# Attention steps of batches 2 to 7 in another order, and k's maxima spread by DMA instead of by TensorE

## The chip, the cores and the metric

One core of one Trainium2 chip runs the whole program. The metric is the device time of one execution in microseconds (us). The kernel before takes 855.56 us, the median of three runs (854.65 to 856.44).

Five engines work side by side, each through its own list of instructions in a fixed order: TensorE (PE in the profile; PEld are its weight loads), VectorE (DVE), ScalarE (ACT), GpSimd (POOL) and SyncE (SP), which here only issues DMAs. An instruction that waits holds up all that stands behind it on its engine.

## The reference

```
q_s = exp(q - max over d);  q_s = q_s / (sum over d + 1e-9)
k_s = exp(k - max over s);  k_s = k_s / (sum over s + 1e-9)
kv  = einsum('bhsd,bhse->bhde', k_s, v)
x   = einsum('bhsd,bhde->bhse', q_s, kv)        # 8 batches, 8 heads, 576 rows, 64 columns
x   = x, heads side by side: 4608 x 512
h   = x @ w_in                                  # 512 -> 2048
out = (h * erf(softplus(h))) @ w_out            # 2048 -> 512
```

Note that k's maximum is taken over the 576 rows, which lie on partitions: it has to be brought to every partition before it can be subtracted.

## The kernel before

**The network (MoE) part** is the bulk of the work. The 4608 tokens are cut into 12 blocks of 384, three for each pair of batches, and the 2048 hidden columns into four groups. One item `n` is one block with one group; there are 48 of them. For an item, `mm1(n, k)` with k = 0 to 3 (L975, matmuls at L999) makes `H_n` in PSUM tiles `pY`, `pX`, `pZ`, each product being 12 matmuls of 128x192; each of the three tiles has one buffer, so a product waits until the one before it in that tile has been read. DVE reads some of them (L1011, L1013, L1021, L1024), ACT the others (L1016, L1018, L1026). Then `softplus` and `erf` run on ACT (L344, each with a table load), `gmul`, `ghi` and `glo` on DVE (L1079, L1093, L1097), and two items later `mm2(n, tt)` with tt = 0 to 2 (L1125, 12 matmuls of 128x512 each) adds into `o`. Operands are split into two fp16 halves, so that three fp16 products stand for one of fp32. The first items (0 to 5) use fp32 for `mm2` (L1116), and while items 4 to 8 run, the weights are still being split (L297, L298) and combined (L322).

**The attention part** makes the tokens `x`, one batch after another. Batches 0 and 1 are written in fp32 and aren't touched by the change. Batches 2 to 7 go through the generator `attention16(b)` (L649), whose steps are:

- `k_max` (L492): DVE takes maxima over each partition's own rows into `kmax`; `k_max_T` (L504): TensorE transposes `kmax` into bank `kT` (L508) and DVE reduces it to `km`, 4 numbers on each of 128 partitions (L512); `k_max_rows` (L517): TensorE transposes `km`, broadcast, into bank `kB` (L521), so that each partition has all 512 maxima in PSUM.
- `q_sub` (L451): row maxima of q and their subtraction (L454, L455); then k minus `kB` (L662, L667), and the exponentials on ACT (L344).
- `kv_mm` and `kv_norm` (L528, L554): k'v of four heads each (`kv_b_0`, `kv_b_1`; L542), its normalization into `kvf` (L565).
- `q_norm` and `q_halves` (L459, L636): q divided by its sums, split into fp16 halves (ACT L640, DVE L641, placed over the k half that k'v has used up), and transposed by a DMA.
- `kv_max` (L576) and `kv_split` (L584): the largest entry of `kvf` (`mx`, L578) is spread over the partitions by a transpose on TensorE into `x_bk` (L125), reduced by DVE (L127), made into a scale, and with it `kvf` is split into `kvbd` (L595, L596), the operand of the next step.
- `x_mm` (L632): for odd batches first the rest of both batches' rows (`xt`), then four products `x_b_0` to `x_b_3`; ACT moves them into the blocks `x` (L443). After `x_b_1` and `x_b_3` the loads of the next batch's q halves are issued, after k'v those of its k and v.

**What sets the order.** After each step the generator yields a share; `pace` (L1207), called after every `mm2`, takes further steps until the sum of shares has reached a goal that rises evenly with `n`. The shares are the table `SHARES16` (L49). The code order this gives is then put through a list scheduler, which fixes each engine's list of instructions by its own estimate of when each is ready. All loads, stores and DMA transposes are issued from SP's one list. The attention banks (`kT`, `kB`, `kv`, `x_bk`, `xt`, `x`) share two PSUM buffers.

The main loop, for items 4 and up:

```
for i in range(4):
    if m0: tok(f"m{n}.{i}")                       # mm1, quarter i of item n
    if 4 < n <= N and i < 2 and n - 1 not in OUT32: tok(f"{'IO'[i]}{n - 1}")
    if m2 and i < 3:
        tok(f"M{n - 2}.{i}")                      # mm2 of item n - 2
        pace(n + (i + 1) / NTT)                   # attention steps
```

Of the kernel before, what the change touches and what calls it, by code (L numbers as in the profile page):

```python
# [45 lines left out]
OUTS = [2, 3, 0, 1]  # L46

SHARES = [2.51, 0, 0.16, 0.09, 1.58, 2.43, 1.12, 0.26, 0.29, 0.04, 0.78, 1.12, 0.16]
SHARES16 = [2.51, 0, 0.16, 0.09, 1.58, 2.43, 1.3, 2.43, 1.3, 0.26, 0.3, 0.78, 0.3]  # L49
LEAD = 2.0  # L50

EXPMASK = 0x7F800000
# [5 lines left out]
def attn_moe_kernel(  # L58
# [18 lines left out]
    NC4 = DM // P  # L77
# [261 lines left out]
    def act(out_, in_, func, chain=True, **kw):  # L339

        with ExitStack() as es:
            if chain and last[0] is not None:
                es.enter_context(tc.issue_after(last[0]))
            i = nc.scalar.activation(out_, in_, func, **kw)  # L344
# [100 lines left out]
    def hd(t):  # L445
        return t.rearrange("p h d -> p (h d)")

    def rows(t):
        return t.rearrange("p t h d -> p (t h) d")

    def q_sub(t, g, name):  # L451

        m = at.tile([P, g], F32, tag=f"qm{g}", bufs=1, name=f"{name}_m")
        nc.vector.tensor_reduce(m, t, axis=AX.X, op=ALU.max)  # L454
        nc.vector.tensor_tensor(  # L455
            t, t, m[:, :, None].to_broadcast([P, g, D]), op=ALU.subtract
        )
# [58 lines left out]

    def k_max_rows(b, km):  # L517

        bk = bank(f"kB_{b}")
        for c in range(NC4):  # L520
            nc.tensor.transpose(  # L521
                bk[:, c * P:(c + 1) * P], km[:, c:c + 1].to_broadcast([P, P]), ident
            )
# [30 lines left out]
    def kv_norm(b, hf, bk):  # L554
        if b >= E32:
            if hf == 0:
                bat[b]["kvf"] = at.tile([P, NC4, D], F32, tag="qT", name=f"kvf_{b}")
            kvf = bat[b]["kvf"]
        bkv = bk[:, :2 * W].rearrange("p (c w) -> p c w", c=2)
        rd = at.tile([P, 2, 1], F32, tag="rd", bufs=1, name=f"rd_{b}_{hf}")  # L560
        nc.vector.tensor_scalar_add(rd, bkv[:, :, D:], 1e-9)
        nc.vector.reciprocal(rd, rd)
        cs = slice(2 * hf, 2 * hf + 2)
        if b >= E32:
            nc.vector.tensor_tensor(  # L565
                kvf[:, cs, :], bkv[:, :, :D], rd.to_broadcast([P, 2, D]), op=ALU.mult
            )
            return
        for a in range(2):
            ps = slice(a * D, (a + 1) * D)  # L570
            nc.vector.tensor_tensor(
                kv32[b][ps, cs, ps], bkv[ps, :, :D], rd[ps].to_broadcast([D, 2, D]),
                op=ALU.mult,
            )

    def kv_max(b):  # L576
        mx = at.tile([P, 1], F32, tag="mx", bufs=1, name=f"mx_{b}")
        nc.vector.tensor_reduce(  # L578
            mx, (kv32[b] if b < E32 else bat[b]["kvf"]).rearrange("p c e -> p (c e)"), axis=AX.X,
            op=ALU.max, apply_absolute_value=True,  # L580
        )
        return mx
# [50 lines left out]
                out_, kvbd[b % 2][:, wl, c, :], qT[:, ql], start=(i == 0), stop=(i == 2)  # L633
            )

    def q_halves(src, place, name):  # L636

        n = src.shape[1]
        st_ = place.bitcast(F16).rearrange("p (i n) -> p i n", i=2)
        nc.scalar.copy(st_[:, 0], src)  # L640
        nc.vector.tensor_tensor(st_[:, 1], src, st_[:, 0], op=ALU.subtract)  # L641
        qT = src.bitcast(F16).rearrange("p (a s) -> p a s", s=P)
        nc.sync.dma_start_transpose(qT, place.bitcast(F16))
        return qT.rearrange("p (i a) s -> p i a s", i=2)

    def flat3(t):
        return t.rearrange("p a b c -> p (a b c)")

    def attention16(b):  # L649
        d, j, p = bat[b], b % 2, b // 2  # L650
        even = bat[b - j]
        tl = slice(j * TAIL, (j + 1) * TAIL)
        ks, qs, kt = d["k"], d["q"], even["kt"][tl]
        sh = iter(SHARES16)
        kmax = k_max(b, ks, (kt, tl))
        yield next(sh)
        km = k_max_T(b, kmax)
        q_sub(rows(qs[0]), 16, f"q_{b}_0")
        yield next(sh)
        kb = k_max_rows(b, km)  # L660
        for hf in range(2):
            nc.vector.tensor_tensor(  # L662
                ks[hf], ks[hf],
                kb[:, None, hf * 4:hf * 4 + 4, :].to_broadcast([P, TM, 4, D]),
                op=ALU.subtract,
            )
        nc.vector.tensor_tensor(kt, kt, kb[tl], op=ALU.subtract)  # L667
        yield next(sh)
        q_sub(rows(qs[1]), 16, f"q_{b}_1")
        if j == 1:  # L670
            q_sub(even["qt"], H, f"qt_{p}")
        yield next(sh)
        for t in (*ks, kt, qs[0], qs[1], *([even["qt"]] if j == 1 else [])):
            act(t, t, AF.Exp, chain=b > 1)
        yield next(sh)
        qT = {}
        for hf in range(2):
            kv_norm(b, hf, kv_mm(b, hf))
            if hf == 0:
                d["v"].append(load_half(v, "v", b, 1))  # L680
            q_norm(rows(qs[hf]), 16, f"q_{b}_{hf}", b)
            yield next(sh)
            qT[hf] = q_halves(flat3(qs[hf]), flat3(ks[hf]), f"{b}_{hf}")
            yield next(sh)
        if j == 1:
            q_norm(even["qt"], H, f"qt_{p}", b)
            qT[2] = q_halves(hd(even["qt"]), hd(even["kt"]), f"{p}_t")
        if b + 1 < B:
            load_kv(b + 1)
        mx = kv_max(b)  # L690
        yield next(sh)
        kv_split(b, mx)
        yield next(sh)
        for i in ((3 * p + 1, 3 * p + 2) if j else (3 * p, 3 * p + 1)):
            while not x_free(i):
                yield 0
        w = next(sh)
        if j == 1:
            bk = bank(f"xt_{p}")
            x = xblock(p * NBK + 1)  # L700
            bk3 = bk.rearrange("p (c s) -> p c s", c=NC4)
            for a in range(2):
                for c in range(NC4):
                    cs = slice(a * TAIL, (a + 1) * TAIL)
# [571 lines left out]
```

## Time and profile before

| | |
|---|---|
| three runs | 854.65, 855.56, 856.44 us |
| the profiled execution | 855.05 us, of which the profile's span is 852.9 us |
| TensorE (PE) | busy 813.8 us, 95% of the span |
| VectorE (DVE) | busy 633.3 us, 74% |
| ScalarE (ACT) | busy 503.5 us, 59% |
| DMA | 62.59 MB, 73 GB/s on average |
| granted TensorE clock | 0.992 |

The span is what the profile can see; 2.1 us of the execution lie around it. An engine's busy share is an average over stages. Items 0 to 3 and batches 0 and 1 fill about the first 130 us, items 4 to 8 with the weights' splitting go to about 205 us, and from there on an item follows an item with batches 2 to 7 woven in, until about 700 us, where the attention has ended and only the network part goes on. Rows of the timeline have the start in us from the span's start, the duration, engine, line, operation, what is written and what is read, and the count of like instructions merged; in square brackets stands how long the engine was idle before it and which instruction released it.

### The profile page before, as it was taken

The page shows a single profiled execution, that of the slowest core. Times are in us where ns is not written, and L with a number is a line of the kernel's source. Part 1 is how long each engine was busy: PE and PEld are TensorE (multiplying, and loading weights), DVE is VectorE, ACT ScalarE, POOL GpSimd, SP SyncE. Part 2 cuts the span into 40 slices and gives each one's busy share as a digit, 9 for nine tenths or more (in the row PEclk, how much of TensorE's full clock was granted, in tenths as well). Part 3 has the DMA queues.
Part 4 walks back from the last instruction along what each step waited for, and adds up shares of the span by engine and source line. Part 5 has one row for each costly group of instructions (what it writes and reads, how often), then busy time and mean ns, then how long its engine had stood idle before and what let it go on. Part 6 is the DMA issues. An engine that isn't in the chain of part 4 may idle for free.

```text
span 852.9 us, 15321 instructions
## 1 busy us (share of the span) xinstructions
PE 813.8 (95%) x6424; PEld 554.2 (65%) x6424; DVE 633.3 (74%) x909; ACT 503.5 (59%) x633; POOL 17.6 (2%) x37
## 2 busy tenths in 40 slices
PE   2999997999999999999999999999999999999997
PEld 1655546666667667766777676766776676777673
DVE  5899979999995879758865779758866656553543
ACT  2598486876674656645663566555664465553532
POOL 2010000000000000000000000000000000000000
PEclk8899999999999999999999999999999999999999
DMA  9996420043326303412134302412131000000100
GB/s 250 409 251 194 123 63 25 7 85 66 87 51 130 98 3 64 99 31 50 49 85 86 91 10 51 97 46 51 33 55 38 31 9 1 38 2 1 38 2 37
DMA packets 145508, 62.59 MB, mean 73 GB/s; under 512 B 134688, under 2 KB 136736, under 8 KB 145440
## 3 DMA queue, kind: packets, MB, share of 16 engines
q1 hardware_dynamic: 143264, 53.23, 25.1%
q0 software_dynamic: 2176, 8.39, 2.7%
q8 instruction: 50, 0.82, 0.4%
q14 instruction: 18, 0.15, 0.1%
HBM read 45.09 MB, written 9.44 MB: 64 GB/s over the span
## 4 chain that ended last, share of the span: by engine, by line
PE 52%; DVE 25%; ACT 14%; issue 4%; SPq 2%; DMA 2%; ACTq 0%; POOL 0%; DVEq 0%
PE o L1125 25%; PE pX L999 13%; PE pZ L999 6%; ACT G L344 6%; ACT L344 5%; DVE G L1079 3%; PE pY L999 3%; DVE H L1097 2%; SPq L409 2%; DVE H L1093 2%; PE kv L542 2%; DVE x L298 1%; PE x L632 1%; DVE x L388 1%; PE o L1116 1%
## 5 line engine op out<-in xcount | busy, mean ns | idle before, releaser
L1125 PE MATMUL o<-wo,H 128*128 128x512 f16 x1512 | 348.0, 379 | 1.7 <-DVE H L1093 1.3
L999 PEld LDWEIGHTS <-wi 128*128 128x128 f16 x3696 | 309.1, 98 | 46.3 <-issue 18.5
L1125 PEld LDWEIGHTS <-H 128*128 128x128 f16 x1512 | 145.7, 98 | 150.0 <-DVE H L1093 1.8
L999 PE MATMUL pX<-x,wi 128*128 128x192 f16 x2112 | 204.8, 247 | 7.7 <-ACT H L1018 4.1
L344 ACT ACT_TABLE_LOAD x104 | 133.4, 1283 | 4.7 <-DVE H L1024 2.8
L1079 DVE SCALAR_TENSOR_TENSOR G<-G,small,H 128x1536 f32<-128x1536 f32 x44 | 80.0, 1817 | 60.9 <-ACT G L344 60.6
L1026 ACT COPY H<-pX 128x384 f32<-128x384 f32 x44 | 20.9, 474 | 163.4 <-PE pX L999 163.4
L999 PE MATMUL pZ<-x,wi 128*128 128x192 f16 x1056 | 103.8, 246 | 1.4 <-DVE H L1024 1.0
L344 ACT ACTIVATE G<-H,U 128x768 f32<-128x768 f32 (+1 forms) x60 | 72.7, 1231 | 22.1 <-DVE H L1024 21.5
L1097 DVE TENSOR_TENSOR H<-G,H 128x1536 f16<-128x1536 f32 x42 | 73.8, 1756 | 1.0
L344 ACT ACTIVATE G<-G 128x1536 f32<-128x1536 f32 x48 | 71.2, 1484 | 0.5
L1116 PE MATMUL o<-wo,G 128*128 128x512 f32 x144 | 66.6, 602 | 0.0
L999 PE MATMUL pY<-x,wi 128*128 128x192 f16 x528 | 51.2, 246 | 1.6 <-DVE H L1011 1.6
L1024 DVE TENSOR_TENSOR H<-pZ,H 128x384 f32<-128x384 f32 x44 | 24.4, 554 | 32.1 <-PE pZ L999 32.1
L1011 DVE COPY H<-pY 128x384 f32<-128x384 f32 x44 | 24.4, 555 | 30.7 <-PE pY L999 30.7
L1116 PEld LDWEIGHTS o<-wo,G 128*128 128x128 f32 x144 | 26.1, 192 | 25.8 <-issue 25.1
L297 ACT ACTIVATE x<-x 128x768 f16<-128x768 f32 (+1 forms) x44 | 32.7, 761 | 14.3 <-DVE x L388 14.2
L1093 DVE CAST H<-G 128x1536 f16<-128x1536 f32 x42 | 40.2, 957 | 0.8
L1141 DVE TENSOR_SCALAR ob<-o,V 128x512 f32<-128x512 f32 x29 | 21.7, 748 | 25.6 <-PE o L1125 25.6
L298 DVE SCALAR_TENSOR_TENSOR x<-x,x 128x768 f16<-128x768 f32 (+1 forms) x44 | 37.1, 852 | 3.4 <-ACT x L297 3.4
L443 ACT ACTIVATE x<-x 128x384 f32<-128x384 f32 (+1 forms) x52 | 17.6, 391 | 32.0 <-PE x L632 29.5
L1013 DVE TENSOR_TENSOR H<-pX,H 128x384 f32<-128x384 f32 x44 | 24.5, 556 | 14.6 <-PE pX L999 14.3
(184 smaller groups left out, 769.0 us busy)
## 6 DMA issues: line engine op xcount, KB each, us to landing
out_dram<-ob SPq DMA_DIRECT2D x32, 256.0 KB, 2.4
vbuf<-in_v_dram SPq DMA_DIRECT2D x60, 128.0 KB, 3.1
q<-in_q_dram SPq DMA_DIRECT2D x56, 128.0 KB, 3.2
k<-in_k_dram SPq DMA_DIRECT2D x56, 128.0 KB, 3.2
wo<-in_moe_w_in_dram SPq DMA_DIRECT2D x4, 1024.0 KB, 17.0
wi<-in_moe_w_out_dram POOLq DMA_DIRECT2D x2, 1024.0 KB, 8.0
wi<-in_moe_w_in_dram SPq DMA_DIRECT2D x2, 1024.0 KB, 8.8
raw<-in_moe_w_out_dram POOLq DMA_DIRECT2D x2, 1024.0 KB, 7.9
```

The costliest lines, as they stand in the source:

```text
L297: nc.scalar.activation(hi, src, AF.Copy, scale=s)
L298: nc.vector.scalar_tensor_tensor(lo, src, s, hi, op0=ALU.mult, op1=ALU.subtract)
L344: i = nc.scalar.activation(out_, in_, func, **kw)
L999: nc.tensor.matmul(o, w[wl][:, c, a * P:(a + 1) * P], x[:, xl, xi, c, :], start=(new and a == 0 and c == 0 and i == 0), stop=(c == 1 and i ...
L1011: nc.vector.tensor_copy(C[0, 0], bank2("Y"))
L1013: add(C[0, 0], bank2("X"), C[0, 0], op=ALU.add)
L1024: add(C[0, 1], bank2("Z"), C[0, 1], op=ALU.add)
L1079: nc.vector.scalar_tensor_tensor(flat(s["G"]), flat(s["G"]), (GB if n in OUT32 else GA)[:, g:g + 1], flat(s["H"]), op0=ALU.mult, op1=ALU.mult,
L1093: nc.vector.tensor_copy(flat(s["gh"]), flat(s["G"]))
L1097: nc.vector.tensor_tensor(flat(s["gl"]), flat(s["G"]), flat(s["gh"]), op=ALU.subtract)
L1116: nc.tensor.matmul(o, s["G"][:, a, ts_], w[:, a, :], start=(first_ and a == 0), stop=(last_ and a == FG - 1),)
L1125: nc.tensor.matmul(o, s[gt][:, a, ts_], w[wl][:, a, :], start=(first_ and a == 0 and i == 0), stop=(last_ and a == FG - 1 and i == 2),)
```

## The change

Three things are changed for batches 2 to 7.

1. `k_max_rows` is replaced by `k_max_spread`: `km` is written by a DMA to a row of 512 numbers in DRAM (4 bytes to a packet), and a second DMA reads that row back, repeated for each of the 128 partitions, into an SBUF tile `kB`. Both are issued from SP, and the second waits for the first. Four transposes on TensorE for each batch go, and the subtraction (now L672, L677) reads SBUF where it read PSUM.
2. The steps stand in another order: maxima, their transposing and the two DMAs are one step; then `q_sub` of both halves, and k's subtraction after them; the first q half stands behind `kv_b_0`, and the second one behind `kv_b_1`, `kv_max` and `kv_split`, which stood behind both q halves.
3. The shares are new numbers, written at each step, and `SHARE16` is their sum.

```
+    def k_max_spread(b, km):
+        row = dr.tile([1, DM], F32, tag="km", name=f"kmd_{b}")
+        nc.sync.dma_start(row.rearrange("o (c p) -> (o p) c", c=NC4), km)
+        kb = at.tile([P, DM], F32, tag="qT", name=f"kB_{b}")
+        nc.sync.dma_start(kb, row.to_broadcast([P, DM]))
+        return kb.rearrange("p (h d) -> p h d", h=H)
...
-        kmax = k_max(b, ks, (kt, tl))
-        yield next(sh)
-        km = k_max_T(b, kmax)
+        kb = k_max_spread(b, k_max_T(b, k_max(b, ks, (kt, tl))))
+        yield 1.8
         q_sub(rows(qs[0]), 16, f"q_{b}_0")
-        yield next(sh)
-        kb = k_max_rows(b, km)
+        yield 0.9
+        q_sub(rows(qs[1]), 16, f"q_{b}_1")
+        if j == 1:
+            q_sub(even["qt"], H, f"qt_{p}")
+        yield 0.9
         for hf in range(2):
             nc.vector.tensor_tensor(
...
+        def q_half(hf):
             q_norm(rows(qs[hf]), 16, f"q_{b}_{hf}", b)
-            yield next(sh)
-            qT[hf] = q_halves(flat3(qs[hf]), flat3(ks[hf]), f"{b}_{hf}")
-            yield next(sh)
+            yield 0.75
+            qT[hf] = q_halves(flat3(qs[hf]), flat3(ks[hf]))
+            yield 0.75
+
+        kv_norm(b, 0, kv_mm(b, 0))
+        d["v"].append(load_half(v, "v", b, 1))
+        yield 0.4
+        yield from q_half(0)
+        kv_norm(b, 1, kv_mm(b, 1))
+        mx = kv_max(b)
+        yield 0.6
+        kv_split(b, mx)
+        yield 0.4
+        yield from q_half(1)
...
-        mx = kv_max(b)
-        yield next(sh)
-        kv_split(b, mx)
-        yield next(sh)
+        yield 0.75 if j == 1 else 0
```

How this moves instructions is shown at three places of batch 5. Names end in a buffer's number, and lines of the changed kernel are some ten higher.

First TensorE around the spreading of `mx`, before. The bank is `x5_bk`, and `kvbd0` and `kvbd1` are the operands that `kv_split` makes of it:

```order
L1125 LDWEIGHTS H_23_4200
L1125 MATMUL o_20_0_4079<-wo2_95,H_23_4200 128x512
L125 MATMUL x5_bk_4582<-ident_76,mx_5_4505 128x128
L632 LDWEIGHTS kvbd0_85
L632 MATMUL xt_2_4599<-qt_2_2542,kvbd0_85 128x64
```

And what stands there in the changed kernel:

```order
L1009 LDWEIGHTS wi3_94
L1009 MATMUL pX_23_4213<-x7_5_3364,wi3_94 128x192
L1135 LDWEIGHTS H_21_3846
L1135 MATMUL o_20_2_4152<-wo0_95,H_21_3846 128x512
L126 MATMUL x5_bk_4267<-ident_78,mx_5_4265 128x128
```

The transpose has moved from item 25 to item 23, between two matmuls of the last `mm2` there, and the products with `kvbd` no longer follow it: `xt_2` now stands in item 24, 106 matmuls later.

Second, VectorE's list ahead of that transpose in the changed kernel, from the item's `gmul` to the reduction of `x5_bk`:

```order
L1089 SCALAR_TENSOR_TENSOR G_22_4194<-G_22_4194,small_83,H_22_4007 128x1536
L570 TENSOR_SCALAR rd_5_1_4261<-kv_5_1_4240 128x2
L1103 CAST H_22_4007<-G_22_4194 128x1536
L571 RECIPROCAL rd_5_1_4261<-rd_5_1_4261 128x2
L650 TENSOR_TENSOR k_5_1_3439<-q_5_1_3621,k_5_1_3439 128x1024
L574 TENSOR_TENSOR kvf_5_4076<-kv_5_1_4240,rd_5_1_4261 128x128
L1107 TENSOR_TENSOR H_22_4007<-G_22_4194,H_22_4007 128x1536
L587 TENSOR_REDUCE mx_5_4265<-kvf_5_4076 128x1
L1031 TENSOR_TENSOR H_23_4198<-pX_23_4213,H_23_4198 128x2x192
L128 TENSOR_REDUCE x5_e_4269<-x5_bk_4267 128x1
```

Before, `mx` and the reduction stood with eleven instructions between them, of which the first seven are:

```order
L578 TENSOR_REDUCE mx_5_4505<-kvf_5_4000 128x1
L1024 TENSOR_TENSOR H_23_4200<-pZ_23_4272,H_23_4200 128x2x192
L1011 COPY H_24_4367<-pY_24_4368 128x2x192
L1013 TENSOR_TENSOR H_24_4367<-pX_24_4382,H_24_4367 128x2x192
L1079 SCALAR_TENSOR_TENSOR G_23_4363<-G_23_4363,small_81,H_23_4200 128x1536
L1093 CAST H_23_4200<-G_23_4363 128x1536
L1097 TENSOR_TENSOR H_23_4200<-G_23_4363,H_23_4200 128x1536
L1021 TENSOR_TENSOR H_24_4367<-pX_24_4382,H_24_4367 128x2x192
```

So the distance between `mx` and its use has shrunk, and that between `kvbd` and its use has grown.

Third, VectorE between `km`, from which the two DMAs start, and the subtraction that needs their result, in the changed kernel:

```order
L513 TENSOR_REDUCE km_5_3663<-kT_5_3658 128x4
L455 TENSOR_REDUCE q_5_1_m_3810<-q_5_1_3621 128x16
L1034 TENSOR_TENSOR H_19_3527<-pZ_19_3575,H_19_3527 128x2x192
L456 TENSOR_TENSOR q_5_1_3621<-q_5_1_3621,q_5_1_m_3810 128x1024
L1021 COPY H_20_3700<-pY_20_3701 128x2x192
L299 SCALAR_TENSOR_TENSOR x7_6_4037<-x_6_3481,x7_6_4037 128x768
L1023 TENSOR_TENSOR H_20_3700<-pX_20_3715,H_20_3700 128x2x192
L389 TENSOR_TENSOR x_6_3481<-x_6_3481 128x2x192
L672 TENSOR_TENSOR k_5_0_3434<-k_5_0_3434,kB_5_3667 128x1024
```

Seven instructions stand between the two; the subtraction waits for the second DMA, and the list behind it waits with it.

More of the change, by code (lines that the diff above doesn't have):

```diff
@@ L48 @@
 SHARES = [2.51, 0, 0.16, 0.09, 1.58, 2.43, 1.12, 0.26, 0.29, 0.04, 0.78, 1.12, 0.16]
-SHARES16 = [2.51, 0, 0.16, 0.09, 1.58, 2.43, 1.3, 2.43, 1.3, 0.26, 0.3, 0.78, 0.3]
+SHARE16 = 1.8 + 0.9 * 3 + 1.5 + 0.4 + 0.75 * 4 + 0.6 + 0.4 + 0.75 * 4
 LEAD = 2.0
@@ L87, in attn_moe_kernel @@
     cp = ctx.enter_context(tc.tile_pool(name="cp", bufs=1))
+    dr = ctx.enter_context(tc.tile_pool(name="dr", bufs=2, space=bass.MemoryType.DRAM))
     ch = ctx.enter_context(tc.tile_pool(name="ch", bufs=1))
@@ L634, in x_mm, with q_halves @@
             )
-    def q_halves(src, place, name):
+    def q_halves(src, place):
         n = src.shape[1]
@@ L653, in attention16 @@
         ks, qs, kt = d["k"], d["q"], even["kt"][tl]
-        sh = iter(SHARES16)
-        kmax = k_max(b, ks, (kt, tl))
-        yield next(sh)
-        km = k_max_T(b, kmax)
+        kb = k_max_spread(b, k_max_T(b, k_max(b, ks, (kt, tl))))
+        yield 1.8
         q_sub(rows(qs[0]), 16, f"q_{b}_0")
-        yield next(sh)
-        kb = k_max_rows(b, km)
+        yield 0.9
[3 more added lines that the diff above has]
+        yield 0.9
         for hf in range(2):
@@ L667, in attention16 @@
         nc.vector.tensor_tensor(kt, kt, kb[tl], op=ALU.subtract)
-        yield next(sh)
-        q_sub(rows(qs[1]), 16, f"q_{b}_1")
-        if j == 1:
-            q_sub(even["qt"], H, f"qt_{p}")
-        yield next(sh)
+        yield 0.9
         for t in (*ks, kt, qs[0], qs[1], *([even["qt"]] if j == 1 else [])):
-            act(t, t, AF.Exp, chain=b > 1)
-        yield next(sh)
+            act(t, t, AF.Exp)
+        yield 1.5
         qT = {}
[L677 to L680, printed above, removed]
+        def q_half(hf):
             q_norm(rows(qs[hf]), 16, f"q_{b}_{hf}", b)
-            yield next(sh)
-            qT[hf] = q_halves(flat3(qs[hf]), flat3(ks[hf]), f"{b}_{hf}")
-            yield next(sh)
+            yield 0.75
[11 more added lines that the diff above has]
+        yield from q_half(1)
         if j == 1:
             q_norm(even["qt"], H, f"qt_{p}", b)
-            qT[2] = q_halves(hd(even["qt"]), hd(even["kt"]), f"{p}_t")
+            qT[2] = q_halves(hd(even["qt"]), hd(even["kt"]))
         if b + 1 < B:
             load_kv(b + 1)
-        mx = kv_max(b)
-        yield next(sh)
-        kv_split(b, mx)
-        yield next(sh)
+        yield 0.75 if j == 1 else 0
         for i in ((3 * p + 1, 3 * p + 2) if j else (3 * p, 3 * p + 1)):
@@ L696, in attention16 @@
                 yield 0
-        w = next(sh)
         if j == 1:
@@ L708, in attention16 @@
                 bat[b + 1]["qt"] = load_tail(q, "qt", p + 1)
-            yield w
-        w = next(sh)
+            yield 0.75
         for c in range(NC4):
@@ L720, in attention16 @@
                 d["xdone"] = True
-            yield w
+            yield 0.75
     def x_split(b, c, bk, part=None):
@@ L1203, in attn_moe_kernel @@
     w_odd = sum(SHARES[:11]) + NC4 * sum(SHARES[11:])
-    per_pair = 2 * (sum(SHARES16[:11]) + NC4 * SHARES16[12]) + SHARES16[11]
+    per_pair = 2 * SHARE16 + 0.75 * 2
     n1 = NG + 3
```

## The prediction

> **What bounds the kernel now.** I read the page's busy shares first, then the busy time by stage, then TensorE's own waits, and last the timeline at the places where attention steps meet the network's. The page's first row, and three stages of the table by windows (columns: us, then busy us of PE, PEld, DVE, ACT, POOL with the number of instructions, granted clock, DMA share, GB/s):
>
> ```profile
> PE 813.8 (95%) x6424; PEld 554.2 (65%) x6424; DVE 633.3 (74%) x909; ACT 503.5 (59%) x633; POOL 17.6 (2%) x37
> ...
> 100.00:150.00 50.00, 44.24 (x265) 28.84 (x264) 43.11 (x76) 39.31 (x58) 1.91 (x2) 1.00 0.16 43
> 150.00:205.00 55.00, 53.82 (x409) 35.61 (x409) 54.08 (x78) 42.78 (x46) 0.63 (x2) 0.97 0.27 58
> 205.00:700.00 495.00, 485.89 (x4234) 342.81 (x4232) 372.48 (x546) 290.24 (x349) 2.52 (x8) 1.00 0.25 58
> ```
>
> From 205 to 700 us TensorE lacks 495.00 - 485.89 = 9.1 us of being busy throughout. It is the bound there; DVE (75%) and ACT (59%) have room, though not at every moment. Before 205 us it is otherwise: from 150 on DVE is as full as TensorE. So a change to the attention of batches 2 to 7 can gain in two ways only: TensorE work that goes, and the 9.1 us of waits. Who causes those waits, in TensorE's table of waits from 205 to 700 us (total us, times, longest):
>
> ```profile
> PE xt L632 <- DVE kvbd L595: 1.9, 3, 0.8
> PE pX L999 <- ACT H L1026: 1.3, 2, 0.6
> PE pX L999 <- DVE H L1021: 1.2, 2, 0.6
> PE pX L999 <- ACT H L1018: 1.1, 1, 1.1
> PE x L632 <- issue: 0.7, 1, 0.7
> PE x L632 <- DVE kvbd L595: 0.7, 2, 0.4
> PE xt L632 <- DVE kvbd L596: 0.6, 1, 0.6
> PE kv L542 <- ACT k L344: 0.5, 1, 0.5
> PE x L632 <- DVE kvbd L596: 0.5, 2, 0.2
> ```
>
> Nearly half hangs on `kvbd`: 1.9 + 0.7 + 0.6 + 0.5, and the 0.7 put down to issue is the first product with `kvbd` too, together 4.4 us. The rest (4.1 us) are banks and exponentials that ACT or DVE bring late.
>
> **The change part by part.** The sum is made against the profiled execution, 855.05 us, which is 0.5 us under the median of 855.56.
>
> *The four transposes to `kB`.* TensorE's timeline around one of them:
>
> ```profile
> 235.07 0.60 PE L521 MATMUL kB<-ident,km 128*128 128x128 f32 x4
> 235.51 1.15 PE L999 MATMUL pX<-x,wi 128*128 128x192 f16 x12
> ```
>
> Rows overlap, so the step from start to start counts: 0.44 us for the four. TensorE is the bound and nothing covers them; six batches give 6 x 0.44 = 2.6 us gained.
>
> *`kv_split` ahead of the second q half.* Now `xt` and `x` stand right behind `kvbd`. In the new order of batch 5 there are 106 matmuls between `x_bk` and `xt`, so the 4.4 us of waits for `kvbd` go. What is late next is `x_bk` itself: its transpose waits for `mx`, which DVE makes behind k'v. I work that out for batch 5, where the new lists are shown. Rows from the same place in an item (23) of before, PE first, then the end of `erf` on ACT, then k'v (20 matmuls of fp32 for half the heads, each as two records):
>
> ```profile
> 469.30 1.15 PE L999 MATMUL pY<-x,wi 128*128 128x192 f16 x12
> ...
> 471.28 2.75 PE L1125 MATMUL o<-wo,H 128*128 128x512 f16 x12
> 473.87 0.27 PE L125 MATMUL x_bk<-ident,mx 128*128 128x128 f32 x1
> ...
> 474.18 1.49 ACT L344 ACTIVATE G<-G 128x1536 f32<-128x1536 f32 x1
> ...
> 420.41 0.69 PE L542 MATMUL kv<-vbuf,k 128*64 128x65 f32 x16
> ...
> 421.73 1.17 PE L999 MATMUL pZ<-x,wi 128*128 128x192 f16 x12
> ```
>
> A product of 12 takes 0.99 us ((471.28 - 469.30)/2), an `mm2` 2.59, k'v 1.32; `erf` ends at 475.67, 6.4 us after the item's start. TensorE's new list from the start of item 23: two products, `mm2`, k'v, two products, `mm2`, one product, two matmuls of the next `mm2` (0.43): 5 x 0.99 + 2 x 2.59 + 1.32 + 0.43 = 11.9 us, and there stands `x_bk`. DVE's list from `erf`'s end, with the mean durations by form:
>
> ```profile
> L1079 DVE SCALAR_TENSOR_TENSOR G<-G,small,H 128x1536 f32<-128x1536 f32 x44 | 80.0, 1817 | 60.9 <-ACT G L344 60.6
> L1097 DVE TENSOR_TENSOR H<-G,H 128x1536 f16<-128x1536 f32 x42 | 73.8, 1756 | 1.0
> L1093 DVE CAST H<-G 128x1536 f16<-128x1536 f32 x42 | 40.2, 957 | 0.8
> ...
> L641 DVE TENSOR_TENSOR k<-q,k 128x1024 f16<-128x1024 f32 x12 | 14.6, 1215 | 0.5 <-ACT k L640 0.5
> ...
> L565 DVE TENSOR_TENSOR kvf<-kv,rd 128x128 f32<-128x128 f32 x12 | 3.3, 274 | 0.0
> ...
> L578 DVE TENSOR_REDUCE mx<-kvf 128x1 f32<-128x256 f32 x6 | 2.4, 406 | 0.1
> ```
>
> That is 1.82 + 0.96 + 1.22 + 0.27 + 1.76 + 0.41 = 6.4 us, so `mx` is there at 6.4 + 6.4 = 12.8 us: TensorE waits some 0.8 us. Batch 7 has the same lists. In batches 4 and 6, where k'v stands behind the second `mm2`, the same count brings TensorE to `x_bk` at 13.9 us and `mx` to 13.7, so no wait; for 3 and 2 I take 0.4 and 0.5, estimates between these two. Cost 2.5 us; bounds 0 and 6 x 0.8 = 4.8.
>
> *The exponentials' place on ACT.* In batches 4 to 7 ACT now copies a `pX` only after a table load and the first exponential; before, that order stood in batches 5 and 7 alone. The 1.1 us for L1018 is one such wait. Against it, two waits for L1026 (1.3 us) lose the DVE work of q that made them. I take nothing, from -1.3 to 3 x 1.1 = +3.3.
>
> *Batch 2, among the weights.* Two q instructions (maxima and subtraction of the second half) have moved ahead of DVE's reading of item 5's third `pX` (L1021), one split of 1.3 us too, and the split of `wo` shown here has moved behind it. DVE, then TensorE:
>
> ```profile
> 146.92 2.36 DVE L298 SCALAR_TENSOR_TENSOR wo<-wo,small,wo 128x2048 f16<-128x2048 f32 x1
> ...
> 152.11 1.29 DVE L298 SCALAR_TENSOR_TENSOR wi<-wi,small,wi 128x1024 f16<-128x1024 f32 x1
> 153.31 0.57 DVE L1021 TENSOR_TENSOR H<-pX,H 128x384 f32<-128x384 f32 x1
> ...
> 150.68 2.08 PE L999 MATMUL pX<-x,wi 128*128 128x192 f16 x12 [3.05 <-ACT H L1018]
> 152.55 3.24 PE L1116 MATMUL o<-wo,G 128*128 128x512 f32 x6
> 155.63 1.15 PE L999 MATMUL pX<-x,wi 128*128 128x192 f16 x12
> ...
> L455 DVE TENSOR_TENSOR q<-q,q_m 128x1024 f32<-128x1024 f32 x14 | 17.2, 1226 | 0.1
> L454 DVE TENSOR_REDUCE q_m<-q 128x16 f32<-128x1024 f32 x14 | 17.1, 1219 | 6.0 <-DMA q<-in_q_dram 6.0
> ```
>
> L1021 ends 1.22 + 1.23 + 1.29 - 2.36 = 1.4 us later, at 155.3. TensorE has one fp32 product fewer ahead of the next `pX` (three took 3.08 us) and no `kB`, so it arrives at 155.63 - 1.0 - 0.44 = 154.2 and waits 1.1 us. Cost 1.1; it could be nothing, or as much as the 3.05 us wait here.
>
> *The two DMAs.* They lie beside other work as long as they land before DVE reaches the subtraction. No row shows a DMA of 4-byte packets to DRAM; the nearest are a load of as many packets (512 of 256 B) and a store of as many bytes as `kB` has (128 packets of 2 KB):
>
> ```profile
> out_dram<-ob SPq DMA_DIRECT2D x32, 256.0 KB, 2.4
> vbuf<-in_v_dram SPq DMA_DIRECT2D x60, 128.0 KB, 3.1
> ...
> L298 DVE SCALAR_TENSOR_TENSOR x<-x,x 128x768 f16<-128x768 f32 x33 | 31.2, 953 | 2.6 <-ACT x L297 2.6
> L1011 DVE COPY H<-pY 128x384 f32<-128x384 f32 x44 | 24.4, 555 | 30.7 <-PE pY L999 30.7
> ```
>
> One after the other: 3.1 + 2.4 = 5.5 us. The cover in batches 5 and 7 is the seven instructions shown: 1.22 + 1.23 + 0.95 + 4 x 0.56 = 5.6 us; in 4 and 6 nine instructions (two of 0.95 us, two of 1.22, five of 0.56) make 7.1; in 2 and 3 more stands between. So I take nothing, from below nothing excluded (the subtraction is no sooner than its place) up to the rival below. On SP, stores and v loads queue behind; their data are due items later. The Trainium skill, "DMA: Bandwidth & Descriptors", section "Anatomy of one DMA", has about 2.0 us fixed for each DMA, most of it the confirmation of the write, heaviest toward HBM; its formula would give the pair an estimated 4.6 us and, like the rows, a cost of nothing. The same page's specifications speak against the first DMA: below 512 B a transfer is read, modified and written.
>
> Sum: -2.6 - 4.4 + 2.5 + 0 + 1.1 + 0 = -3.4 us: 851.65 for such an execution, 852.2 for the median.
>
> **The rivals.** *More is gained:* DVE and ACT keep ahead, so `x_bk`, batch 2 and the exponentials cost nothing: -2.6 - 4.4 - 1.3 = -8.3, 847.3 us. For it speaks DVE's 25% of idle time, against it the waits of before, which are of this kind.
>
> *The waits only move:* every `x_bk` waits 0.8 us (2.3 more than taken) and every batch from 4 on repeats the 1.1 us of L1018 (3.1 more net). Half of that is -3.4 + 2.7 = -0.7: 854.9 us, no measurable change.
>
> *Slower: the DMA pair lands late.* DVE stands at the subtraction with `gmul` behind it, and TensorE then waits for `H`. With a pair of 10 us and about 1 us of slack, batches 5 and 7 lose 10 - 5.6 - 1 = 3.4 us each, 4 and 6 lose 1.9: 10.6 in all, 862.8 us. It is slower by more than 0.2% from the point where 2(W - 6.6) + 2(W - 8.1) = 3.4 + 1.7, a pair of W = 8.6 us. The page's read-modify-write rule would work in this direction. Against it: the loads of 512 packets land in 3.1 us.
>
> That the change does not do what it says I exclude: the new lists have no transposes to `kB` from batch 2 on.
>
> **How the numbers follow.** Below 0.2% (1.7 us) a measurement of this kernel can't tell a change from none. Chances: forecast 0.48, more gained 0.17, only moved 0.21, slower 0.14. Faster takes 0.44 of the forecast's case, all of the second and 0.03 of the third: 0.64; slower takes 0.14 and 0.01 of the third: 0.15; the rest, 0.21, is no change. The range from 847.5 to 857.0 takes in the forecast with its bounds and the moved waits, and leaves out the late DMAs and the far end of the larger gain.
>
> **What would show it.** Right: from 205 to 700 us no wait for `kvbd`, waits for `mx` at `x_bk` (new, up to 1 us each), no row L521 for later batches, the pair landing within about 6 us, no idle DVE at k's subtraction. Wrong: DVE waiting for `kB`, or waits for L1018 in four batches that eat the gain, or a first 205 us that end over 3 us later.

## The result, and the profile after

The changed kernel takes 899.68 us (median of four runs, 897.93 to 900.91) beside 855.11 us for the kernel before (854.58 to 856.44): a ratio of 1.0518, 95% interval 1.0500 to 1.0535. It is slower by 44.6 us, where I had forecast 3.4 us less.

The page's first row of the changed kernel, and its window from 205 to 700 us (columns as before: us, then busy us of PE, PEld, DVE, ACT, POOL with their instructions, granted clock, DMA share, GB/s):

```profile
PE 822.9 (92%) x6400; PEld 561.9 (63%) x6400; DVE 635.8 (71%) x909; ACT 504.2 (56%) x633; POOL 17.6 (2%) x37
```

```profile
205.00:700.00 495.00, 449.61 (x3843) 319.51 (x3842) 349.80 (x510) 265.17 (x314) 2.53 (x8) 0.97 0.27 61
```

TensorE does 24 matmuls less and is nevertheless busy 9.1 us longer, at a granted clock of 0.97 in this stretch (1.00 before). Where it lacked 9.1 us of being busy throughout, it now lacks 495.00 - 449.61 = 45.4. The first 205 us, in which batch 2 stands, are not the place: TensorE is busy 180.58 us there, and was 181.13 before, with 21 matmuls fewer by then (1042 for 1063).

Who causes the waits, in TensorE's table of waits from 205 to 700 us (total us, times, longest):

```profile
PE pX L1009 <- DVE H L1031: 27.6, 4, 8.1
PE x_bk L126 <- DVE mx L587: 10.8, 4, 5.0
PE pX L1009 <- DVE H L1023: 3.0, 1, 3.0
PE kT L509 <- DVE kmax L502: 1.6, 1, 1.6
```

No wait names `kvbd` any more, as forecast. But there are 27.6 us for `H`, one wait in each of batches 4 to 7, and 10.8 us for `mx`; the 3.0 us for L1023 are batch 3's, of the same origin. Why `H` is late shows in the groups of VectorE's instructions, where k's subtraction now has idle time before it (after the bar: busy us, mean ns of one, idle us before them and what ended it), and in the DMA issues (last column: median us from issue to landing):

```profile
L672 DVE TENSOR_TENSOR k<-k,kB 128x1024 f32<-128x1024 f32 x12 | 14.3, 1220 | 31.9 <-DMA kB<-kmd 31.9
...
kB<-kmd SPq DMA_DIRECT2D x6, 256.0 KB, 4.8
...
kmd<-km SPq DMA_DIRECT2D x6, 2.0 KB, 7.9
```

The pair takes 7.9 + 4.8 = 12.7 us, where I had reckoned 5.5. The timeline of batch 5, first SP's list, then VectorE's, then TensorE's, has it in one view:

```profile
408.43 0.38 SPq L530 DMA_DIRECT2D kmd<-km  x1
416.75 0.33 SPq L532 DMA_DIRECT2D kB<-kmd  x1
...
407.71 0.69 DVE L513 TENSOR_REDUCE km<-kT 128x4 f32<-128x512 f32 x1 [2.40 <-PE kT L509]
...
413.29 0.55 DVE L389 TENSOR_TENSOR x<-x 128x384 f32<-128x384 f32 x1
421.57 2.36 DVE L672 TENSOR_TENSOR k<-k,kB 128x1024 f32<-128x1024 f32 x2 [7.73 <-DMA kB<-kmd]
...
425.61 1.81 DVE L1089 SCALAR_TENSOR_TENSOR G<-G,small,H 128x1536 f32<-128x1536 f32 x1
...
430.81 0.55 DVE L1031 TENSOR_TENSOR H<-pX,H 128x384 f32<-128x384 f32 x1
...
422.21 1.15 PE L1009 MATMUL pZ<-x,wi 128*128 128x192 f16 x12
431.42 2.08 PE L1009 MATMUL pX<-x,wi 128*128 128x192 f16 x12 [8.05 <-DVE H L1031]
433.29 1.79 PE L1009 MATMUL pY<-x,wi 128*128 128x192 f16 x12
434.91 1.15 PE L1009 MATMUL pX<-x,wi 128*128 128x192 f16 x12
```

The maxima are ready at 408.4. The second DMA is issued 8.3 us after the first, for which it waits, and lands 4.8 us later. VectorE's work in between ends at 413.8, it stands for 7.73 us, and everything queued behind (`gmul`, the casts, L1031) is late by that much: TensorE waits 8.05 us. Then its next products run slowly, 2.08 and 1.79 us for 1.15. Such a stretch, in batch 4, in the table by windows (the third figure from the end is the granted clock):

```profile
318.60:325.30 6.70, 5.77 (x37) 5.44 (x37) 3.57 (x5) 3.60 (x4) 0.00 (x0) 0.50 0.00 0
```

The second group, `mx`, in batch 4, VectorE and then TensorE:

```profile
364.74 0.69 DVE L498 TENSOR_TENSOR k<-k 128x512 f32<-128x512 f32 x1 [5.07 <-DMA k<-in_k_dram]
365.35 1.81 DVE L1089 SCALAR_TENSOR_TENSOR G<-G,small,H 128x1536 f32<-128x1536 f32 x1
...
370.60 1.22 DVE L650 TENSOR_TENSOR k<-q,k 128x1024 f16<-128x1024 f32 x1
...
372.57 0.42 DVE L587 TENSOR_REDUCE mx<-kvf 128x1 f32<-128x256 f32 x1
...
373.05 0.42 PE L126 MATMUL x_bk<-ident,mx 128*128 128x128 f32 x1 [4.81 <-DVE mx L587]
...
373.68 2.13 PE L1009 MATMUL pZ<-x,wi 128*128 128x192 f16 x12
```

L498 is batch 5's first k maximum. The scheduler has put it ahead of batch 4's `mx`, and there it stands 5.07 us for k's load, with `gmul` and `mx` behind it.

### The profile page after: what moved, and what is told of

Read it like the earlier page. It is cut to its first block, busy times and chain, and to the rows that moved or that the text cites. A ratio compares the mean times of both kernels' runs of the same rounds, so it can differ in the third digit from the quotient of the medians.

```text
span 898.6 us, 15288 instructions
## 1 busy us (share of the span) xinstructions
PE 822.9 (92%) x6400; PEld 561.9 (63%) x6400; DVE 635.8 (71%) x909; ACT 504.2 (56%) x633; POOL 17.6 (2%) x37
## 4 chain that ended last, share of the span: by engine, by line
PE 49%; DVE 25%; DMA 14%; ACT 4%; SPq 3%; issue 3%; ACTq 0%; DVEq 0%
PE o L1135 22%; PE pX L1009 13%; PE pZ L1009 6%; DMA kmd<-km 4%; PE pY L1009 3%; DVE G L1089 3%; SPq L410 3%; DMA kB<-kmd 3%; DMA k<-in_k_dram 2%; PE o L1126 2%; DMA q<-in_q_dram 2%; DMA q<-k 2%; DVE H L1107 2%; ACT G L345 2%; DVE x L299 1%
## 5 line engine op out<-in xcount | busy, mean ns | idle before, releaser
L1009 PEld LDWEIGHTS <-wi 128*128 128x128 f16 x3696 | 318.6, 100 | 75.4 <-issue 47.1
L1009 PE MATMUL pX<-x,wi 128*128 128x192 f16 x2112 | 210.5, 251 | 36.3 <-DVE H L1031 28.5
L1009 PE MATMUL pY<-x,wi 128*128 128x192 f16 x528 | 54.4, 255 | 0.6 <-DVE H L1021 0.6
L298 ACT ACTIVATE x<-x 128x768 f16<-128x768 f32 (+1 forms) x44 | 32.8, 760 | 25.2 <-DVE x L389 25.0
L672 DVE TENSOR_TENSOR k<-k,kB 128x1024 f32<-128x1024 f32 x12 | 14.3, 1220 | 31.9 <-DMA kB<-kmd 31.9
```

The source lines that it names most:

```text
L298: nc.scalar.activation(hi, src, AF.Copy, scale=s)
L1009: nc.tensor.matmul(o, w[wl][:, c, a * P:(a + 1) * P], x[:, xl, xi, c, :], start=(new and a == 0 and c == 0 and i == 0), stop=(c == 1 and i ...
```

## The experiments

Ratios are to the kernel before, run beside them, with 95% intervals. Theory 1 is the late pair, theory 2 the new order, theory 3 the pair's hold on SP's list.

### The order or the DMAs: e1 and e2

e1 is the changed kernel without its DMAs:

```
-        kb = k_max_spread(b, k_max_T(b, k_max(b, ks, (kt, tl))))
+        km = k_max_T(b, k_max(b, ks, (kt, tl)))
         yield 1.8
...
         yield 0.9
+        kb = k_max_rows(b, km)
         for hf in range(2):
             nc.vector.tensor_tensor(
                 ks[hf], ks[hf],
```

> The new order alone: k's maxima reach all partitions by TensorE's four transposes again, right ahead of k's subtraction; no DMA is added. Theory 1 (the DMA pair, some 12.5 us from the maxima to the landing where I had reckoned 5.5, holds DVE at k's subtraction, and TensorE waits for H behind it): DVE's 31.9 us of waits for kB and TensorE's 28.5 us for L1031 go, and the granted clock returns to 1.00; 850 to 858 us. Theory 2 (the order itself is dear: k's loads land late, which was 25.0 us of DVE's waits, and x_bk waits 10.8 us for mx): most of the loss stays, 875 us or more.

858.76 us, ratio 1.0053 (1.0036 to 1.0070). Nine tenths of the loss is gone, so theory 2 falls as the main cause; but some 4.5 us slower is left, just beyond what theory 1 had allowed. TensorE's waits from 205 us on, then the row of VectorE's:

```profile
PE x_bk L126 <- DVE mx L587: 5.6, 4, 2.7
PE pX L1010 <- DVE H L1032: 3.9, 4, 2.7
...
DVE k L498 <- DMA k<-in_k_dram: 17.9, 8, 3.3
```

The 2.7 us of them in batch 4, on TensorE's timeline, with the slow product behind it:

```profile
357.97 0.47 PE L126 MATMUL x_bk<-ident,mx 128*128 128x128 f32 x1 [2.74 <-DVE mx L587]
358.24 2.13 PE L1010 MATMUL pZ<-x,wi 128*128 128x192 f16 x12
```

e2 is the kernel before with the pair in place of its transposes to `kB`, issued where those to `kT` stand (the definition of `k_max_spread` is left out here):

```
-        km = k_max_T(b, kmax)
+        kb = k_max_spread(b, k_max_T(b, kmax))
         q_sub(rows(qs[0]), 16, f"q_{b}_0")
         yield next(sh)
-        kb = k_max_rows(b, km)
...
```

> The DMAs alone: the order of before, with the pair issued where the transposes to kT stand, and of the work that covered it only q's first maxima and subtraction (2.4 us) still between. Theory 1: DVE stands 12.5 - 2.4 = about 10 us at k's subtraction in each of six batches, of which TensorE feels some 7 to 9 in each: 895 to 915 us. Theory 2: about the time of before, below 865 us, since k's loads and x_bk are where they were.

906.48 us, 1.0618 (1.0603 to 1.0634), as theory 1 had it. VectorE waits 47.7 us for `kB`, up to 11.7 each, with the old order. TensorE feels it mostly through k'v, which stood right behind the exponentials of k:

```profile
PE kv L551 <- ACT k L345: 25.6, 4, 8.2
...
DVE k L670 <- DMA kB<-kmd: 47.7, 5, 11.7
```

### What the pair's time is made of: e3, e4, e5

e3 writes the same 2 KB as 128 packets of 16 bytes instead of 512 of 4:

```
-        nc.sync.dma_start(row.rearrange("o (c p) -> (o p) c", c=NC4), km)
+        nc.sync.dma_start(row.rearrange("o (p c) -> (o p) c", c=NC4), km)
...
-        return kb.rearrange("p (h d) -> p h d", h=H)
+        return kb.rearrange("p (a d c) -> p c a d", a=2, c=NC4)
...
```

The subtractions are written anew to fit, four of half the size for two.

> The changed kernel, but each partition writes its four maxima as one packet of 16 bytes (128 packets for 512); DVE reads kB with a step of four elements, in four subtractions of half the size for two. If the time of the first DMA (7.5 us) goes with the number of packets: 2 to 4 us for it, DVE's waits for kB fall from 31.9 us to below 10, and the time to 860 to 875 us. If it is latency or queueing that does not depend on them: 7 us or more again, and 895 to 902 us (a few us more if the reading with a step is slow).

875.86 us, 1.0261 (1.0245 to 1.0276), just above the first answer. Its DMA issues, and the subtraction's row (shortest, median and longest duration in ns, first and last start):

```profile
kB<-kmd SPq DMA_DIRECT2D x6, 256.0 KB, 3.3
kmd<-km SPq DMA_DIRECT2D x6, 2.0 KB, 2.5
...
L673 DVE TENSOR_TENSOR k<-k,kB x24: 1068/1096/1201, 159.9 to 613.4; 128x512 f32<-128x512 f32 x24
```

The pair falls from 12.7 to 5.8 us, and VectorE's waits for `kB` from 31.9 to 0.8. So the time goes with the 4-byte packets, not with a latency that any DMA to DRAM would have; the read, whose own packets are the same, is 1.5 us shorter too. Yet the packets themselves are quickly moved. The changed kernel's batch 5 by windows, from the write's packets to the read's (last three columns: granted clock, DMA share, GB/s):

```profile
409.30:409.90 0.60, 0.60 (x10) 0.60 (x8) 0.60 (x2) 0.21 (x1) 0.00 (x0) 1.00 0.45 4
409.90:416.70 6.80, 6.80 (x61) 5.03 (x60) 3.94 (x7) 6.74 (x8) 0.00 (x0) 1.00 0.03 1
416.75:419.50 2.75, 2.75 (x21) 1.69 (x20) 0.00 (x0) 1.19 (x3) 0.00 (x0) 1.00 0.00 0
```

By this table the 2 KB are moved within 0.6 us, and 6.8 us more pass with next to nothing moved until the write counts as landed. The read, issued at 416.75, moves nothing before 419.5; in e3 it starts 1.1 us after its issue. What these times are spent on, the trace doesn't show.

What is left of e3's loss may in part be this experiment's own price: a half-size subtraction with a step of four elements takes 1096 ns, nearly as much as a whole one (1220), and VectorE is busy 649.5 us instead of 635.8.

e4 lets the read not wait for the write:

```
-        nc.sync.dma_start(kb, row.to_broadcast([P, DM]))
+        src = q[b, 0:1, 0:H, :].rearrange("o s d -> o (s d)")
+        nc.sync.dma_start(kb, src.to_broadcast([P, DM]))
```

> The changed kernel, but kB is read from a row of q in DRAM instead of the row just written, so that the read need not wait for the write (what is subtracted from k is then not its maximum). The write is still made. Theory 1: kB lands about 5 us after it is issued, inside the 5.6 us of cover, DVE does not wait for it, and the time is 850 to 862 us. Theory 2: DVE's waits for kB go all the same, but the time stays above 875 us.

867.32 us, 1.0152 (1.0128 to 1.0177): between the two answers. The experiment did more than I meant. Since `kB` no longer hangs on the maxima, the scheduler moved the subtraction ahead even of them, as batch 5 shows:

```profile
382.56 2.35 DVE L673 TENSOR_TENSOR k<-k,kB 128x1024 f32<-128x1024 f32 x2
400.72 0.69 DVE L513 TENSOR_REDUCE km<-kT 128x4 f32<-128x512 f32 x1 [2.40 <-PE kT L509]
```

It shows that most of the loss goes with the waiting (3.0 us for `kB` are left), and that something dear remains which is not the waiting: `x_bk` waits 11.1 us here. Its read, of a row that no DMA had just written, lands after 3.4 us.

e5 is e1 with the pair issued besides, and nobody reading what it brings:

```
         km = k_max_T(b, k_max(b, ks, (kt, tl)))
+        k_max_spread(b, km)
```

> The kernel of e1 (new order, maxima spread by TensorE), and the two DMAs are issued besides, with nobody reading what they bring. It prices what the pair does without being waited for: SP's wait of 7.5 us for its own first DMA, with loads queued behind. Theory 1 (the pair costs only through DVE's waiting for kB): as e1, ratio to before 1.003 to 1.008. Theory 3 (part of the loss is that the pair holds up SP's list, so that k's loads land later): 862 us or more, ratio 1.010 or more, with more than 17.9 us of DVE's waits for k's loads.

859.47 us, 1.0050 (1.0031 to 1.0069), as e1, and k's loads are no later (18.0 us of waits). Theory 3 falls: SP's standing 8 us for its own first DMA costs nothing that these runs can tell.

### The place of the subtraction: e6 and e11

In e1 the subtraction stands 22 instructions behind the maxima on VectorE's list of batch 5, in the changed kernel 8, though the shares are the same: it seems that the list scheduler took `kB` to be there early. e6 keeps the pair and holds the subtraction back, by tiny matmuls that read k first:

```
         yield 0.9
+        pin = bank(f"pin_{b}")
+        for i, t in enumerate((ks[0][:, 0, 0, :], ks[1][:, 0, 0, :], even["kt"][:, 0, :])):
+            nc.tensor.matmul(pin[:D, i * 8:i * 8 + 8], t, t[:, :8], start=True, stop=True)
         for hf in range(2):
             nc.vector.tensor_tensor(
                 ks[hf], ks[hf],
```

> The changed kernel with its own shares, but three tiny matmuls (64x8) read k ahead of its subtraction, so that the subtraction keeps the place that it has with TensorE's transposes, some 27 us behind the maxima instead of 8 DVE instructions behind. The pair is the same, 12.5 us, but covered. Theory 1 (the place of the subtraction, which the scheduler moved up because it took kB to be there early, makes the pair's lateness dear): DVE's 31.9 us for kB go to 0, and with the 2.6 us of TensorE's transposes saved the time is that of e1 or 1 to 3 us less: ratio 1.001 to 1.005. Theory 3 (SP held up): 860 us or more. If the pair itself were dear wherever it stands: 880 or more.

856.00 us, 1.0019 (1.0004 to 1.0033). The same pair, as slow as ever (8.2 and 4.9 us), and 0.0499 of the 0.0518 is gone. VectorE never waits for `kB`; TensorE's largest waits from 205 us on are

```profile
PE pX L1012 <- DVE H L1034: 4.4, 5, 1.7
PE x_bk L126 <- DVE mx L587: 3.6, 4, 1.4
```

The tiny matmuls (`pin`, each as two records) have a price, which I had not reckoned. TensorE in batch 5 of e6:

```profile
414.82 0.40 PE L673 MATMUL pin<-k 128*64 128x8 f32 x4
415.07 0.26 PE L673 MATMUL pin<-kt 128*64 128x8 f32 x2
415.26 1.16 PE L1012 MATMUL pZ<-x,wi 128*128 128x192 f16 x12
```

From start to start they take 0.44 us, as much as the four transposes to `kB` that the pair replaces. So the kernels with them (e6, e8, e10, e13) save TensorE next to nothing.

e11 asks what the early place costs by itself: TensorE's transposes right behind the maxima, so that `kB` is there at once and the subtraction early.

```
-        kb = k_max_spread(b, k_max_T(b, k_max(b, ks, (kt, tl))))
+        kb = k_max_rows(b, k_max_T(b, k_max(b, ks, (kt, tl))))
```

> The new order with TensorE's transposes to kB right behind the maxima in the first step: no DMA, and kB is there at once, so that VectorE's list has k's subtraction as early as in the changed kernel (2 to 10 instructions behind the maxima). It prices the early place by itself. If it is the place that costs the 9 to 13 us that e4 lost more than e1 and e6: ratio 1.012 to 1.018, with some 11 us of waits for mx at x_bk. If those were the DMAs' doing: ratio 1.003 to 1.008, as e1.

865.97 us, 1.0134 (1.0103 to 1.0165), as expected if the place itself is dear. It is earlier still than in the changed kernel: in batches 4 to 7 the subtraction stands 4 instructions behind the maxima, there 8 or 11. Again the waits for `mx` are the large ones (TensorE's, then VectorE's row for k's loads):

```profile
PE x_bk L126 <- DVE mx L587: 10.0, 4, 5.0
...
DVE k L498 <- DMA k<-in_k_dram: 22.9, 9, 5.2
```

Work done early on VectorE brings it sooner to the next batch's maxima, whose load is no earlier; so it stands there longer, ahead of `mx`. e12 tests that reading, though at the late place; at the early one it was not tested.

### The gains that were forecast: e7, e8, e10

e7 is the kernel before with one part of the change, the second q half behind `kv_split`:

```
             if hf == 0:
                 d["v"].append(load_half(v, "v", b, 1))
+            else:
+                mx = kv_max(b)
+                yield 0.26
+                kv_split(b, mx)
+                yield 0.3
             q_norm(rows(qs[hf]), 16, f"q_{b}_{hf}", b)
...
```

> Before with one part of the change: the second q half moved behind kv_1, kv_max and kv_split; shares, first steps and TensorE's transposes as before. My prediction's terms for this part were -4.4 us (waits for kvbd) and +2.5 us (new waits for mx at x_bk): -1.9 us, ratio 0.998. Against it, by e1: waits for mx of 5.6 us and more, since VectorE's list has the next batch's first k maxima, which wait for k's loads, ahead of mx: +2 to +5 us, ratio 1.002 to 1.006. If the cost of e1 came from the other steps and shares, this one is at 0.996 to 0.999.

854.04 us, 0.9995 (0.9978 to 1.0012): neither the forecast 0.998 shown nor excluded, a loss of 0.2% excluded. `kvbd` has left the table of waits (4.4 us before), and these have come:

```profile
PE x_bk L125 <- DVE mx L578: 3.2, 4, 1.4
PE pX L1002 <- DVE H L1024: 2.9, 6, 1.2
```

e8 is the kernel before with the pair alone, issued 2.2 shares ahead of the subtraction, which the tiny matmuls of e6 hold in its place:

```
         kmax = k_max(b, ks, (kt, tl))
-        yield next(sh)
-        km = k_max_T(b, kmax)
+        yield next(sh) - 2.2
+        kb = k_max_spread(b, k_max_T(b, kmax))
+        yield 2.2
         q_sub(rows(qs[0]), 16, f"q_{b}_0")
...
```

> Before with the DMAs alone, but early and covered: the maxima are transposed and the pair is issued 2.2 shares ahead of k's subtraction, which the three tiny matmuls hold at its place of before; six batches lose their four transposes to kB. Theory 1: the pair is hidden (some 15 us of cover), and 6 x 0.44 less some 6 x 0.1 for the tiny matmuls = 2 us are gained: 851 to 853 us beside 854 to 855, ratio 0.9965 to 0.9990. Theory 3 (SP held up): slower than before, ratio 1.005 or more.

854.27 us, 0.9990 (0.9977 to 1.0003): hidden, as theory 1 says, and VectorE never waits for `kB`. That there is no more gain than the measurement can tell fits the price of the tiny matmuls. e10 is e7 and e8 together.

> The two parts that did not hurt, together: e8 (the pair early, the subtraction held at its place of before) and e7 (second q half behind kv_split), with the shares of before. Alone they had ratios 0.999 and 0.9995. If their gains add: 0.997 to 0.999, which would beat both kernels. If the waits for mx at x_bk grow, since VectorE's list is fuller there: 1.000 to 1.003.

853.95 us, 0.9996 (0.9980 to 1.0013): the gains don't add, or are too small to be seen.

### The slow products: e9

e9 is the changed kernel with 44 matmuls that nobody reads, in the four items where TensorE waits for L1031, to keep it busy there:

```
             add(C[0, 1], bank2("Z"), C[0, 1], op=ALU.add)
+            if n in (14, 20, 26, 32):
+                z = ident.bitcast(F16)
+                busy = psh.tile([P, 512], F32, tag="pY", name=f"busy_{n}")
+                for _ in range(44):
+                    nc.tensor.matmul(busy[:, :256], z[:, :P], z, start=True, stop=True)
             prod("X", 2, 4)
```

> The changed kernel, and in items 14, 20, 26 and 32 TensorE does 44 matmuls of 128x256 that nobody reads (some 4.8 us) where it stands waiting for VectorE's L1031 (5.5 to 8 us each). VectorE's list and the DMA pair are the same. If the granted clock falls because TensorE stands idle (behind those waits three products took 5.7 us together instead of 3.0): no fall there, and more work makes it faster by up to 4 x 2.7 = 11 us: 889 to 895 us, ratio 1.040 to 1.047. If the fall has another cause: 898 to 902 us as the changed kernel, ratio 1.050 or more.

898.03 us, 1.0518 (1.0490 to 1.0546). The gain in time that idleness as the cause had let expect did not come. In the rows the theory holds, TensorE in batch 4, then in batch 5:

```profile
311.31 4.97 PE L1039 MATMUL busy<-ident 128*128 128x256 f16 x44
317.13 1.15 PE L1009 MATMUL pX<-x,wi 128*128 128x192 f16 x12 [0.84 <-DVE H L1031]
...
418.45 4.97 PE L1039 MATMUL busy<-ident 128*128 128x256 f16 x44
426.95 1.65 PE L1009 MATMUL pX<-x,wi 128*128 128x192 f16 x12 [3.53 <-DVE H L1031]
428.39 2.13 PE L1009 MATMUL pY<-x,wi 128*128 128x192 f16 x12
```

Where 0.84 us of idleness was left, there is no slow product; where 3.53 us were left, there is. Filling helped in two of the four places only, and the next wait, for `mx`, brings its own slow products. From the maxima to `x_bk` batch 4 went from 74.3 to 71.1 us and batch 6 from 74.8 to 72.9, but batch 5 from 69.7 to 70.1 and batch 7 from 69.6 to 70.2. So the 9.1 us of longer busy time can't be taken as a loss that would go if TensorE were kept busy; how much of it a stall really costs stays open.

### The next batch's maxima: e12 and e13

e12 is e1 with two one-column copies that keep the next batch's first maxima behind `kv_split`:

```
         k2 = at.tile([P, 2, 4, D], F32, tag="qT", name=f"k2_{b}")
+        if b > E32:
+            nc.vector.tensor_copy(k2[:, 0, 0, 0:1], kvbd[(b - 1) % 2][:, 0, 0, 0:1])
+            nc.vector.tensor_copy(k2[:, 0, 0, 1:2], kvbd[(b - 1) % 2][:, 1, 3, P - 1:P])
```

> The kernel of e1 (new order, maxima spread by TensorE), but two one-column copies from kvbd into the next batch's k2 keep that batch's first maxima behind kv_split on VectorE's list, where they stood ahead of mx and waited there for k's loads. If the order's cost in e1 (ratio 1.0053) comes from those waits ahead of mx: x_bk's waits fall from 5.6 us to below 2, the slow products behind them go, and the ratio is 0.998 to 1.001. If the load wait merely moves to another place ahead of something that TensorE needs, or the cost lies in the other steps: 1.003 to 1.007.

851.91 us beside 854.13, 0.9975 (0.9963 to 0.9986): faster than both kernels. The wait of `x_bk` in batch 4 is down from 2.74 us in e1 to 0.40, and the product behind it is not slow. First TensorE's total from 205 us on, then the timeline:

```profile
PE x_bk L126 <- DVE mx L590: 1.8, 4, 0.5
...
355.28 0.32 PE L126 MATMUL x_bk<-ident,mx 128*128 128x128 f32 x1 [0.40 <-DVE mx L590]
...
355.87 1.15 PE L1013 MATMUL pZ<-x,wi 128*128 128x192 f16 x12
```

So the order's cost in e1 came from these maxima standing ahead of `mx`: holding them back is worth 0.0053 + 0.0025 = 0.0078, or 6.7 us, for 3.8 us of waits in the table and what follows from them.

e13 is e6 with the same copies.

> The kernel of e6 (changed kernel with k's subtraction held at its late place) with the same copies. If both causes are met, the waits for kB (0) and those for mx (3.6 us in e6, below 1.5 here) are gone and TensorE's transposes saved: ratio 0.996 to 0.999, faster than before. If not: as e6, 1.001 to 1.003.

854.58 us, 0.9998 (0.9986 to 1.0011): missed. `x_bk`'s waits are down to 2.4 us and none is for `kB`, yet it is 2.0 us slower than e12, which still has TensorE's transposes. The 2.6 us that I had expected the DMAs to save go to the tiny matmuls. For the rest the two profiles show a wait of 2.1 us for the maxima at `kT` and one of 0.8 us at `x`, which e12's does not have; that these make the difference was not tested.

## Why the prediction was wrong

The loss of 0.0518 parts by differences of ratios, times 855 us: the new order with TensorE's transposes (e1) 0.0053, 4.5 us; the early place of the subtraction (e11 less e1) 0.0081, 6.9 us; the pair landing late at that place (the changed kernel less e11) 0.0384, 32.8 us, net of the transposes saved. The last two are rough, since e11's place is not quite the same one; together, 0.0465, they are what e1 shows.

**The two DMAs, the step that failed.** I took nothing for them, with 3.1 us for the first DMA, from "a load of as many packets", and 2.4 for the second. They took 7.9 and 4.8. The analogy was wrong in kind: the load's 512 packets hold 256 bytes each and go to SBUF, these hold 4 and go to DRAM; with 16 bytes to a packet the same data took 2.5 us. The cover I counted was right (seven instructions, 5.6 us; measured from 408.4 to 413.8, 5.4). The mechanism stood among my rivals, with its turning point at a pair of 8.6 us, and got 0.14. There the price was too small: for a pair of 12.7 us my formula, with 1 us of slack, gives 2 x 6.1 + 2 x 4.6 = 21.4 us, and no such slack existed (in batch 5 VectorE is 7.73 us late, TensorE 8.05). In batch 3, where I had counted on more cover, VectorE still stood for 3.7 us and TensorE for 3.0.

The Trainium skill, "DMA: Bandwidth & Descriptors", section "Anatomy of one DMA", gave the pair an estimated 4.6 us, by a formula that the page fits to DMAs issued from GpSimd, while this pair goes out from SP; the trace has 12.7, so a fixed cost of some 2.0 us with bytes over bandwidth does not hold for this pair. The rule of its specifications on transfers below 512 bytes points the right way, but 16 bytes are below 512 too, and took 2.5 us.

**`x_bk`, mis-sized.** Forecast 2.5 us: 0.8 each in batches 5 and 7 (by its own terms, 12.8 less 11.9, it should have been 0.9), none in 4 and 6. Batches 5 and 7 measured 0.5 each; 4 and 6 measured 4.81 and 4.99. My list of VectorE's work ahead of `mx` held only instructions with their durations; one of them, L498, was itself waiting for a load. I had asked of each moved step what it waits for, but not of its new neighbours.

**What held.** The waits for `kvbd` went (e7 and the changed kernel alike). The exponentials' place cost nothing (no wait for ACT's copies of `pX` among those shown). Batch 2, forecast at 1.1 us, cost some 1.6 by an estimate: beside the same matmuls of `mm2`, at 108.1 and 210.4 us before, the changed kernel is 0.85 and 3.36 us behind, and of the 2.5 us between, six `x` products more and four transposes fewer make 0.9; the clock also stands at 0.50 for 6.8 us there instead of 3.4. And the order, once L498 stands behind `mx`, is a gain, as the forecast without DMAs and transposes had it: -0.8 us forecast, -2.1 measured in e12.

**Not tested: the transposes' 2.6 us.** e6 is 2.9 us faster than e1, but not by them, since its tiny matmuls take as long; its waits for `mx` are 2.0 us shorter, and the slow product behind one of them is gone. No run shows the pair hidden and TensorE's work saved.

**Not foreseen: what a stall does to the clock.** Behind the long waits products take up to 1.9 times as long (2.13 us for 1.15) for some microseconds, at a granted clock of 0.50.

## What to carry to other kernels

Ask of a DMA on a path how many packets it has and of how many bytes, and take its time only from one of the same kind; a scheduler that takes a DMA to be faster than it is may move its reader up and expose the lateness, as it seems to have done here. When an instruction moves on an engine that works in order, check what the instructions ahead of it wait for, not only how long they run. A transfer that is covered costs nothing that e8 could measure, even at 13 us, so hold its reader back before making it faster, and count what the holding costs.

## What the runs showed of the hardware

- A write of 2 KB from SBUF to DRAM takes 7.9 us (median) as 512 packets of 4 bytes and 2.5 us as 128 of 16. The read that repeats this 2 KB row for 128 partitions takes 4.8 us behind the first and 3.3 behind the second. Packet number and size changed together, so which of them counts wasn't told apart. In batch 5 of the changed kernel 6.8 of the write's 8.3 us come after its packets have been moved.
- VectorE reading one fp32 operand with a step of four elements took 1096 ns for 128x512, where a packed 128x1024 takes 1220.
- TensorE's granted clock falls from 1.00 to 0.50 behind long waits, and products take up to 2.13 us instead of 1.15 (changed kernel, batch 4, 318.6 to 325.3 us). In the traces of all these runs, from 205 us on, no wait up to 2.06 us brought it and every one from 3.27 us on did. Between, some did (2.18 us in e4, 2.74 in e1) and some did not (2.77 in e3, 3.03 in the changed kernel's batch 3); the same wait of 2.69 us in batch 3 did in e5 and did not in e1 and e12. The Trainium skill, "TensorE: Matmul & The Clock Gate", section "Part 1: The HAM clock gate", has the clock halved after an idle window of about 3.4 us that runs freely; the trace agrees on the halving, but waits shorter than that window were enough in some places.
